# Block 0's root on ScalarE and VectorE, Mish's table loaded behind it, and k, v of batches 2 and 3 on 96 partitions

## The chip, the cores and the metric

The kernel runs on one core of a Trainium2 chip. Measured is the time of one execution on the device in microseconds (us); a comparison takes several executions of each kernel on the same chip. The core's engines are PE (TensorE, matrix products; PEld are its weight loads), DVE (VectorE), ACT (ScalarE), POOL (GpSimd) and SP (SyncE, which here only issues DMAs). Each runs its own instructions strictly in their order and waits on semaphores for the others.

## The reference

A linear attention without softmax gives 2304 rows of 512, and two feed-forward layers follow, the first with Mish, the second with a gated softmax and a normalization:

```python
kv = np.einsum('bhsd,bhse->bhde', k, v)            # batch 4, heads 8, seq 576, dim 64
out = np.einsum('bhsd,bhde->bhse', q, kv)
rms = np.sqrt(np.mean(out * out, axis=-1, keepdims=True) + 1e-06)
x = (out / rms * g_norm)                           # -> 2304 x 512

h = x @ w_in                                       # 512 -> 2048
sp = np.where(h > 20.0, h, np.log1p(np.exp(np.minimum(h, 20.0))))
x = (h * np.tanh(sp)) @ w_out                      # Mish, 2048 -> 512

h = x @ w2_in                                      # 512 -> 1024
e = np.exp(h - np.max(h, axis=-1, keepdims=True))
solu = h * (e / (np.sum(e, axis=-1, keepdims=True) + 1e-09))
ln = (solu - mu) / np.sqrt(var + 1e-06) * g_ln
return ln @ w2_out                                 # 1024 -> 512
```

## The kernel before

The 2304 rows are cut into six blocks of 384 (three tiles `r` of 128 rows each). Float32 operands of the big products are split into two float16 parts, high and low, and a product is three passes over such parts. Three stages follow each other on PE: attention and the first layer (`h_mm` at line 739, with shorter forms from line 833 on), mixed with the layer's second product (line 907), then the second layer (lines 1016 and 1162).

Every piece of work is a task with a key, an engine, a cost and the tasks that it comes after. The table `SEQUENCE` holds the order in which all tasks are written out, which is the order of each engine's instructions; nothing is reordered at run time. `plan.timed` replays the order with the tasks' costs. Where this replay has a gap on PE, `keep_warm` (line 1707) puts in matmuls of 256 columns whose result nobody reads.

The opening, about the first 30 us, is what the change is about. For each batch the eight heads' k and v come in four loads of two heads (`load_pair`, DMAs at line 346), and `kv_pair` (line 379) multiplies them into `kvp`. For batches 0 and 1 (`WIDE`) a head lies on 64 partitions, so that two heads' products run side by side on the halves of the array: 9 rows, 18 matmuls for a pair. For batches 2 and 3 the first 512 of 576 positions lie on 128 partitions (4 rows, 8 matmuls) and the other 64 come by loads of their own (`load_rest`, line 336), on 64 partitions, for 2 matmuls more. `kv_full` (line 384) copies `kvp` to `kvf`, the lower half on ACT and the upper on DVE.

For blocks 0 and 1 a tile then goes through this chain: `t_q` turns q (line 441, PE), `t_xo` multiplies it with `kvf` (line 453, PE), `a_sq` squares (line 497, ACT), `a_ms` sums over a head (line 502, DVE), `a_ep` adds 1e-6 (line 506, POOL), `a_rho` raises to the power -0.5 (line 512, POOL), `a_xf` scales the tile (line 518, DVE), `t_x` turns it (line 461, PE), and `t_xhi` and `t_xlo` (lines 466 ACT and 471 DVE) make the two halves `xT`, which `h_mm` reads. The first products `H0` are done tile by tile, 12 matmuls of 128 columns each.

The weights come in pieces of 512 KB (line 551 for `w_in`) through five buffers `st`. A piece is unpacked by `w_scale` (line 598, ACT), `w_sign` (line 603, POOL), `w_low` (608, DVE), `w_put` (615, DVE), `w_hi` (626, ACT) and `w_lo` (635, DVE). All loads stand in SP's one queue.

## Time and profile before

| what | us |
|---|---|
| median of 3 runs (579.33 to 579.74) | 579.49 |
| profiled execution, its own time | 579.91 |
| span of the profiled execution | 578.1 |
| PE busy in it | 571.4 (99%) |
| DVE, ACT, POOL busy | 441.2, 367.4, 129.3 |

The profile page gives an engine's busy time and its share of the span. The timeline gives each instruction's start and length, the number of equal ones that are merged, and in brackets the engine's idle time before it with what ended it. Float32 matmuls are done in two passes, and products of 64 or 128 columns with different operands then show as two instructions: a pair of heads, 18 matmuls in the program, shows as 36.

### The profile page before, as it was taken

How to read it: one execution, taken by the hardware profiler on the slowest of the kernel's cores; microseconds unless marked ns; L12 is line 12 of the kernel's file. 1: busy time of each engine (PE TensorE's matmuls, PEld its weight loads, DVE VectorE, ACT ScalarE, POOL GpSimd, SP SyncE). 2: the span in 40 equal slices, each digit the busy share in tenths (PEclk: the TensorE clock that was granted, in tenths of full speed). 3: DMA queues.
4: the chain of work that ended last, by engine and by line, in shares of the span. 5: the costliest groups of instructions: out<-in, count | busy, mean ns of one | idle time of the engine just before them, and what ended most of it. 6: DMA issues, size and time to landing. Idle time of an engine off the chain costs nothing.

```text
span 578.1 us, 12245 instructions
## 1 busy us (share of the span) xinstructions
PE 571.4 (99%) x4920; PEld 413.8 (72%) x4920; DVE 441.2 (76%) x745; ACT 367.4 (64%) x636; POOL 129.3 (22%) x185
## 2 busy tenths in 40 slices
PE   8999999999999999999999999999999999999997
PEld 7886666666678877887777787774545557677886
DVE  2899898899958978787573876996575998697851
ACT  2688666675737643364645567774769797888841
POOL 1766422331022301101100101000305305234300
PEclk9999999999999999999999999999999999999999
DMA  8996979928505380225114232281056448676995
GB/s 317 367 237 169 250 207 323 238 84 177 80 1 75 38 248 12 69 93 177 62 73 157 82 128 84 83 289 48 1 137 183 91 74 164 130 163 135 219 221 155
DMA packets 132090, 84.42 MB, mean 146 GB/s; under 512 B 96450, under 2 KB 119362, under 8 KB 131778
## 3 DMA queue, kind: packets, MB, share of 16 engines
q1 hardware_dynamic: 131888, 83.58, 56.7%
q8 instruction: 38, 0.62, 0.4%
q14 instruction: 18, 0.15, 0.1%
q10 hardware_dynamic: 146, 0.07, 0.0%
HBM read 46.67 MB, written 12.06 MB: 102 GB/s over the span
## 4 chain that ended last, share of the span: by engine, by line
PE 96%; DMA 2%; SPq 0%; issue 0%; DVE 0%; ACT 0%; POOL 0%; POOLq 0%; DVEq 0%
PE y L907 33%; PE hp L833 19%; PE h L1016 14%; PE op L1162 13%; PE hp L739 11%; PE kvp L379 2%; PE xo L481 2%; DMA yT<-in_v_dram 1%; DMA w<-ws 1%; PE hp L1707 1%; PE xo L453 1%; PE xTp L461 0%; PE qTp L441 0%; SPq L346 0%; DVE kvf L384 0%
## 5 line engine op out<-in xcount | busy, mean ns | idle before, releaser
L907 PE MATMUL y<-g,w 128*128 128x384 f16 x1152 | 202.5, 326 | 0.0
L907 PEld LDWEIGHTS <-w 128*128 128x128 f16 x1152 | 110.7, 98 | 66.9
L603 POOL TENSOR_SCALAR st<-st 128x512 f32<-128x512 f32 x48 | 41.0, 858 | 211.0 <-ACT P L598 201.0
L1162 PEld LDWEIGHTS <-w 128*128 128x128 f16 x768 | 74.1, 98 | 12.8 <-DMA w<-ws 0.6
L1162 PE MATMUL op<-yT,w 128*128 128x256 f16 (+1 forms) x576 | 72.4, 271 | 0.4 <-DMA w<-ws 0.4
L889 DVE SCALAR_TENSOR_TENSOR g<-m,g 128x768 f16<-128x768 f32 x48 | 45.8, 961 | 15.4 <-ACT g L884 15.1
L739 PEld LDWEIGHTS <-w 128*128 128x128 f16 x480 | 41.2, 98 | 21.3
L833 PEld LDWEIGHTS <-w 128*128 128x128 f16 x576 | 48.4, 98 | 3.7
L833 PEld LDWEIGHTS <-ws 128*128 128x128 f16 x576 | 48.5, 98 | 3.4
L739 PE MATMUL hp<-xT,w 128*128 128x384 f16 (+1 forms) x384 | 49.8, 286 | 0.0
L608 DVE SCALAR_TENSOR_TENSOR st<-st 128x512 int32<-128x512 int32 x48 | 33.5, 706 | 13.7 <-POOL st L603 13.6
L598 ACT ACTIVATE P<-st 128x512 f32<-128x512 f32 x48 | 32.1, 671 | 16.1 <-DMA st<-in_moe_w_in_dram 7.8
L1071 POOL TENSOR_SCALAR small<-small 128x1 f32<-128x1 f32 x18 | 13.0, 720 | 131.6 <-ACT e L1053 131.2
L884 ACT ACTIVATE g<-m 128x768 f16<-128x768 f32 x48 | 39.9, 838 | 3.7 <-PE y L907 3.5
L1016 PEld LDWEIGHTS <-w 128*128 128x128 f16 x210 | 20.6, 98 | 22.3
L1016 PE MATMUL h<-st,w 128*128 128x512 f16 x150 | 35.0, 379 | 0.0
L615 DVE SCALAR_TENSOR_TENSOR P<-P,st 128x512 int32<-128x512 int32 x48 | 33.1, 703 | 1.0
L512 POOL TENSOR_TENSOR rho<-ms,nhalf 128x8 f32<-128x8 f32 x18 | 31.0, 1727 | 1.0
L1162 PE MATMUL op<-ws,w 128*128 128x256 f16 (+1 forms) x192 | 31.1, 271 | 0.0
L850 ACT ACTIVATE st<-hp 128x384 f32<-128x384 f32 x32 | 15.5, 485 | 24.2 <-PE hp L833 24.2
L833 PE MATMUL hp<-xT,ws 128*128 128x192 f16 x336 | 30.8, 246 | 0.0
L1016 PEld LDWEIGHTS <-ws 128*128 128x128 f16 x168 | 16.4, 98 | 17.7
(164 smaller groups left out, 1007.0 us busy)
## 6 DMA issues: line engine op xcount, KB each, us to landing
st<-in_moe_w_in_dram SPq DMA_DIRECT2D x24, 512.0 KB, 6.1
st<-in_moe_w_out_dram SPq DMA_DIRECT2D x24, 512.0 KB, 5.1
w_far<-F SPq DMA_DIRECT2D x15, 256.0 KB, 2.4
qraw<-in_q_dram SPq DMA_DIRECT2D x4, 768.0 KB, 6.2
w_far<-st SPq DMA_DIRECT2D x11, 256.0 KB, 2.6
out_dram<-yT SPq DMA_DIRECT2D x11, 256.0 KB, 2.4
yT<-w_far SPq DMA_DIRECT2D x3, 896.0 KB, 4.9
st<-w_far SPq DMA_DIRECT2D x5, 512.0 KB, 7.1
```

What stands on the lines that cost most here:

```text
L512: nc.gpsimd.tensor_tensor(out=rho, in0=ms, in1=nhalf, op=ALU.pow)
L598: nc.scalar.activation(out=P, in_=v[:, :, 1], func=ACTF.Copy, scale=2.0 ** -111)
L603: nc.gpsimd.tensor_scalar(out=v[:, :, 1], in0=v[:, :, 1], scalar1=0.0, scalar2=1.0, op0=ALU.mult, op1=ALU.mult)
L608: nc.vector.scalar_tensor_tensor(out=v[:, :, 0], in0=v[:, :, 0], scalar=29, in1=v[:, :, 1], op0=ALU.logical_shift_right, op1=ALU.bitwise_or)
L615: nc.vector.scalar_tensor_tensor(out=P.bitcast(I32), in0=P.bitcast(I32), scalar=3, in1=v[:, :, 0], op0=ALU.logical_shift_left, op1=ALU.bit ...
L739: nc.tensor.matmul(out=h_t[b, grp, i][:, t], lhsT=w1[:, f, c, wa], rhs=xT_t[b][:, C * xa + c, t], start=(c == 0 and m == 0), stop=(c == C ...
L833: nc.tensor.matmul(out=p[:, HT * fs:HT * fs + HT], lhsT=lhsT, rhs=x[:, C * xa + 2 * kx + c, HT * n:HT * n + HT], start=(opens and fs == 0 ...
L884: nc.scalar.activation(out=g_t[b, grp][:, 0, 2 * i:2 * i + 2], in_=m_t[b, grp, i], func=ACTF.Copy, scale=64.0)
L889: nc.vector.scalar_tensor_tensor(out=g_t[b, grp][:, 1, j], in0=m_t.pop((b, grp, i)), scalar=64.0, in1=g_t[b, grp][:, 0, j], op0=ALU.mult, ...
L907: nc.tensor.matmul(out=y_t[cc][:, 0:BLK], lhsT=w2[:, grp * G + ii, wa, cc * 128:(cc + 1) * 128], rhs=g_t[b, grp][:, ga, ii], start=(first ...
L1016: nc.tensor.matmul(out=T[p, "2" + bank], lhsT=yF[p][:, x, ya, c], rhs=w3[w][:, c, wa], start=(first and m == 0), stop=(m == 5), skip_group ...
L1162: nc.tensor.matmul(out=T[p, bank][:, lo:hi], lhsT=lnTs[p % 2][:, 8 * x + 4 * la + kk], rhs=w4[kk][:, 7 * HB * wa + HB * w + lo:7 * HB * wa ...
```

## The change

Three things change, and with them the table of the order.

For block 0 the tasks `ep` and `rho` on POOL go. In their place `a_rt` takes the square root on ACT, with 1e-6 as the bias, and `a_recip` the reciprocal on DVE. Block 1 and the blocks after it keep POOL's power. ACT begins with the table for the square root instead of Mish's; a new task `tab` loads Mish's table after the three roots and ahead of the first Mish.

For batches 2 and 3 a head's 576 positions lie on 96 partitions in 6 rows: `load_rest` goes, and a pair is 12 matmuls of 96 partitions.

The table `SEQUENCE` is new up to the middle of the first stage; from there on PE's instructions stand as before. The number of `keep_warm` matmuls is 47 where it was 37.

```diff
 SEQUENCE = """
-442 2164 481 2165 447 443 448 501 514 502 449 527 503 463 450 515 464 516 7 444 465 445 14 466 451 528
+442 2163 0 2164 479 443 447 448 499 512 500 14 501 463 1 449 2 464 450 444 513 15 445 3 514 525 16 7 465
...
+    K1, K2R = 2 * S // 128, S // 96
+    eps = const.tile([128, 1], FP32, name="eps")
...
     def load_pair(b, i):
-        t = raw_of(b, i)[:, 0:2 * K1 * D].rearrange("p (a r d) -> p a r d", a=2, r=K1)
+        t = yT[RAW[b][i]].rearrange("p c a t -> p (c a t)").bitcast(FP32)
+        if b in WIDE:
+            t = t[:, 0:2 * K1 * D].rearrange("p (a r d) -> p a r d", a=2, r=K1)
+        else:
+            t = t[0:96].rearrange("p (a h r d) -> p a h r d", a=2, h=2, r=K2R)
         raw[b, i] = t
         for a, src in enumerate((k, v)):
             s = src[b, 2 * i:2 * i + 2]
...
+            s = s.rearrange("h (p r) d -> (h p) r d", r=K1) if b in WIDE else s.rearrange(
+                "h (p r) d -> p h r d", r=K2R)
+            nc.sync.dma_start(out=t[:, a], in_=s)
...
-        n = K1 if b in WIDE else 5
+        n = K1 if b in WIDE else K2R
         for r in range(n):
             for h in range(2):
...
+                kh, vh = (t[HALF[h], a, r] if b in WIDE else t[:, a, h, r] for a in range(2))
...
+    def a_rt(b, r):
+        rho = at.tile([128, H, 1], FP32, tag="rho", name="rho", bufs=3)
+        nc.scalar.activation(out=rho, in_=ms_t[b, r], func=ACTF.Sqrt, bias=eps)
+        rho_t[b, r] = rho
+
+    def a_recip(b, r):
+        ms_t.pop((b, r))
+        nc.vector.reciprocal(out=rho_t[b, r], in_=rho_t[b, r])
...
-            task(("ep", *u), "G", 0.25, a_ep, u, [("ms", *u)])
-            task(("rho", *u), "G", 1.7, a_rho, u, [("ep", *u)] + ring("rho", 3, ("xf", *u)))
+            if b:
+                task(("ep", *u), "G", 0.25, a_ep, u, [("ms", *u)])
+                task(("rho", *u), "G", 1.7, a_rho, u, [("ep", *u)] + ring("rho", 3, ("xf", *u)))
+            else:
+                task(("rt", *u), "A", 0.22, a_rt, u, [("ms", *u)] + ring("rho", 3, ("xf", *u)))
+                task(("rho", *u), "V", 0.2, a_recip, u, [("rt", *u)])
...
+    task(("tab",), "A", 1.4, nc.scalar.preload_act_table_set, ("mish",), [("rt", 0, r) for r in range(R)])
...
-    nc.scalar.preload_act_table_set("mish")
+    nc.scalar.preload_act_table_set("sqrt_and_others")
+    nc.vector.memset(eps, 1e-6)
```

What the new table does to the order is seen at three places. SP's queue, from its first load on, before (`qraw` is block 0's q, `yT` holds the raw k and v, `st` a weight piece):

```order
L357 DMA qraw<-in_q_dram 128x8x192
L346 DMA yT<-in_k_dram 128x576
L346 DMA yT<-in_v_dram 128x576
L346 DMA yT<-in_k_dram 128x576
L346 DMA yT<-in_v_dram 128x576
L346 DMA yT<-in_k_dram 128x576
L346 DMA yT<-in_v_dram 128x576
L346 DMA yT<-in_k_dram 128x576
L346 DMA yT<-in_v_dram 128x576
L551 DMA st<-in_moe_w_in_dram 128x4x256 x2
```

The same place after the change:

```order
L544 DMA st<-in_moe_w_in_dram 128x4x256
L346 DMA qraw<-in_q_dram 128x8x192
L339 DMA yT<-in_k_dram 128x576
L339 DMA yT<-in_v_dram 128x576
L339 DMA yT<-in_k_dram 128x576
L339 DMA yT<-in_v_dram 128x576
L544 DMA st<-in_moe_w_in_dram 128x4x256
L339 DMA yT<-in_k_dram 128x576
L339 DMA yT<-in_v_dram 128x576
L339 DMA yT<-in_k_dram 128x576
L339 DMA yT<-in_v_dram 128x576
L544 DMA st<-in_moe_w_in_dram 128x4x256
```

One weight piece now stands at the very front and a second between the pairs of batch 0; the third follows directly behind the last pair.

ACT, from q's copies to the second square, before (`P<-st` is the scaling of a weight piece):

```order
L447 ACTIVATE qT<-qTp 128x512 x2
L384 COPY kvf<-kvp 64x4x64
L598 ACTIVATE P<-st 128x512
L447 ACTIVATE qT<-qTp 128x512
L497 ACTIVATE sq<-xo 128x512
L388 ACTIVATE kvr_95<-kvf 64x4x64 x2
L497 ACTIVATE sq<-xo 128x512
```

And after the change, up to the second root:

```order
L431 ACTIVATE qT<-qTp 128x512
L591 ACTIVATE P<-st 128x512 x2
L431 ACTIVATE qT<-qTp 128x512
L591 ACTIVATE P<-st 128x512
L368 COPY kvf<-kvp 64x4x64
L431 ACTIVATE qT<-qTp 128x512
L619 ACTIVATE w_70<-P,gs 128x4x128
L481 ACTIVATE sq<-xo 128x512 x2
L495 ACTIVATE rho<-ms,eps 128x8
L481 ACTIVATE sq<-xo 128x512
L495 ACTIVATE rho<-ms,eps 128x8
```

Three scalings of weight pieces have moved ahead of the copy of `kvf`.

PE, from batch 0's last pairs to the first `H0`, before (`ident` alone is `keep_warm`, eleven times here):

```order
L379 MATMUL kvp<-yT 64x64 x36
L441 MATMUL qTp<-ident,qf 128x128 x4
L453 MATMUL xo<-kvf,qT 128x128 x12
L379 MATMUL kvp<-yT 64x64 x36
L461 MATMUL xTp<-ident,xf 128x128 x4
L1707 LDWEIGHTS ident
L1707 MATMUL hp<-ident 128x256
...
L461 MATMUL xTp<-ident,xf 128x128 x4
L441 MATMUL qTp<-ident,qf 128x128 x4
L379 MATMUL kvp<-yT 64x64 x36
L461 MATMUL xTp<-ident,xf 128x128 x4
L441 MATMUL qTp<-ident,qf 128x128 x4
```

And from `xo` on after the change:

```order
L437 MATMUL xo<-kvf,qT 128x128 x12
L363 MATMUL kvp<-yT 64x64 x18
L425 MATMUL qTp<-ident,qf 128x128 x4
L445 MATMUL xTp<-ident,xf 128x128 x4
L363 MATMUL kvp<-yT 64x64 x18
L425 MATMUL qTp<-ident,qf 128x128 x4
L445 MATMUL xTp<-ident,xf 128x128 x4
L732 LDWEIGHTS w_70
```

The first `H0` now follows the second turned tile, not the third; the third turned tile and batch 1's last two pairs stand between the first `H0`s, and no `keep_warm` is left behind `xo`.

## Rows read from the trace of the kernel before

**Rows 1.** The page: busy time, share of the span, instructions; clock in 40 slices.

```profile
PE 571.4 (99%) x4920; PEld 413.8 (72%) x4920; DVE 441.2 (76%) x745; ACT 367.4 (64%) x636; POOL 129.3 (22%) x185
PEclk9999999999999999999999999999999999999999
```

**Rows 2.** Waits of PE in the whole span: who waited for whom, total, times, longest.

```profile
PE kvp L379 <- DMA yT<-in_v_dram: 0.8, 3, 0.4
PE xTp L461 <- DVE xf L518: 0.6, 2, 0.4
```

**Rows 3.** Timeline of PE, opening: start, length, line, operation, count, idle before.

```profile
7.61 1.26 PE L379 MATMUL kvp<-yT 64*64 64x64 f32 x36
8.81 0.66 PE L441 MATMUL qTp<-ident,qf 128*128 128x128 f32 x4
...
10.74 2.38 PE L379 MATMUL kvp<-yT 64*64 64x64 f32 x72
13.05 0.66 PE L441 MATMUL qTp<-ident,qf 128*128 128x128 f32 x4
14.10 2.94 PE L453 MATMUL xo<-kvf,qT 128*128 128x128 f32 x24 [0.40 <-ACT kvf L384]
16.99 1.26 PE L379 MATMUL kvp<-yT 64*64 64x64 f32 x36
18.44 1.26 PE L379 MATMUL kvp<-yT 64*64 64x64 f32 x36 [0.19 <-DMA yT<-in_v_dram]
...
20.42 1.36 PE L1707 MATMUL hp<-ident 128*128 128x256 f16 x11
22.15 0.66 PE L461 MATMUL xTp<-ident,xf 128*128 128x128 f32 x4 [0.37 <-DVE xf L518]
...
26.51 0.63 PE L461 MATMUL xTp<-ident,xf 128*128 128x128 f32 x4
26.97 0.60 PE L441 MATMUL qTp<-ident,qf 128*128 128x128 f32 x4
27.41 0.83 PE L739 MATMUL hp<-xT,w 128*128 128x128 f16 x12
```

**Rows 4.** Timeline of the other engines, chain from the square to the power.

```profile
15.30 0.60 ACT L497 ACTIVATE sq<-xo 128x512 f32<-128x512 f32 x1 [0.20 <-PE xo L453]
16.01 0.68 DVE L502 TENSOR_REDUCE ms<-sq 128x8 f32<-128x512 f32 x1
17.07 1.67 POOL L512 TENSOR_TENSOR rho<-ms,nhalf 128x8 f32<-128x8 f32 x1
19.18 0.69 DVE L518 SCALAR_TENSOR_TENSOR xf<-xo,rho 128x512 f32<-128x512 f32 x1
```

**Rows 5.** Stretches of the opening: busy time by engine, clock, DMA share, GB/s.

```profile
5.00:10.00 5.00, 5.00 (x74) 4.07 (x74) 1.19 (x3) 1.10 (x2) 0.00 (x0) 1.00 1.04 407
15.00:20.00 5.00, 4.59 (x92) 4.22 (x91) 3.98 (x7) 3.88 (x8) 3.34 (x6) 1.00 1.08 364
35.00:40.00 5.00, 5.00 (x61) 4.21 (x59) 4.96 (x9) 4.15 (x9) 2.40 (x4) 1.00 0.74 259
```

**Rows 6.** Timeline of ACT and DVE, the copy, a scaling, a small copy, q's.

```profile
6.08 0.76 DVE L435 COPY qf<-qraw 128x512 f32<-128x512 f32 x2 [3.38 <-DMA qraw<-in_q_dram]
...
10.84 0.16 DVE L1292 COPY gs<-hp 128x1 f32<-128x1 f32 x1 [2.76 <-PE hp L1289]
...
13.68 0.37 ACT L384 COPY kvf<-kvp 64x256 f32<-64x256 f32 x1 [3.59 <-DVE kvf L384]
13.95 0.66 ACT L598 ACTIVATE P<-st 128x512 f32<-128x512 f32 x1
```

**Rows 7.** Groups of ACT's instructions: the table loads, busy, mean ns, idle before.

```profile
L1695 ACT ACT_TABLE_LOAD x1 | 1.3, 1283 | 0.7 <-PEq L1752 0.7
```

**Rows 8.** Timeline of PE at batch 2's first pair.

```profile
91.59 0.95 PE L379 MATMUL kvp<-yT 128*64 128x64 f32 x20
92.47 0.82 PE L907 MATMUL y<-g,w 128*128 128x384 f16 x4
```

34 lines of the change are left out of this document (4 added, 30 removed), and 186 rows, old and new, of the table SEQUENCE.

## The prediction

> **What bounds the kernel now.** I read the page's busy times first, then the waits of PE, then the timeline of the opening. PE is busy 99% of the span at a granted clock of 0.9 or more in every slice [rows 1], and its waits for operands in the whole run come to little: the two largest kinds for data are 0.8 us for k and v and 0.6 us for the scaled tile, and both lie in the opening [rows 2, 3]. Once the first `H0` has begun at 27.41 us [rows 3] PE is one closed stream, so the end moves with two things only: when that stream gets going, and how much work is in it. A root that is ready sooner is worth nothing by itself. It is worth what it takes out of PE's opening.
>
> In the opening the reader is to see three things. From the first `xo` at 14.10 to the first `H0` at 27.41 [rows 3], 13.31 us pass. The transfers run without a pause, 364 to 407 GB/s [rows 5], so that what PE needs next is there when its turn in the one queue comes. And POOL's power takes 1.67 us [rows 4] for each of three tiles, between a sum and a scaling of 0.7 us each.
>
> **Which work stands where.** By the order of the instructions, PE does the same things ahead of the first `xo` in both kernels (three turns of q, the four pairs of batch 0, the turn of g), apart from fill. Behind it the rest is the same too, with the eleven fill matmuls gone. So I take the first `xo` as the mark: the change in time is the shift of that mark, less the waits and fill that lie behind it now and then no more, plus new waits, plus the change of the work itself.
>
> **What is removed behind the mark.** The 13.31 us hold this work [rows 3]: `xo` 2.89 us (14.10 to 16.99), four pairs of batch 1 at 1.20 us (7.61 to 8.81 is one alone), three turned tiles at 0.46 us (26.51 to 26.97) and two turns of q at 0.44 us (26.97 to 27.41). That is 2.89 + 4.80 + 1.38 + 0.88 = 9.95 us. The other 3.36 us are waits for k and v, waits for the tile that POOL's power holds back, and fill; the stretch of fill alone, from 20.42 to 22.15, is 1.73 us. The whole 3.36 us can go, and no more than that.
>
> **The shift of the mark.** The first `xo` needs both copies of `kvf`. On ACT its copy now stands behind the scaling of the third weight piece, and that waits for its load, which stands behind 768 KB of q, two other pieces of 512 KB and eight loads of k and v of 288 KB. 768 + 3 x 512 + 8 x 288 = 4608 KB must be in. Before, ACT's copy at 13.68 [rows 6] waited for no piece, and only 768 + 8 x 288 = 3072 KB had to come. When are 4608 KB in? PE's wait for v ended just before 18.44 [rows 3], when 768 + 2 x 512 + 12 x 288 = 5248 KB had come. 640 KB less, at 364 GB/s [rows 5] or 355 KB per us, is 1.8 us earlier: 16.6 us. From the other side, q's 768 KB are in at 6.08 [rows 6]; the 3840 KB behind them take 9.7 us at 407 GB/s and 10.8 at 364 [rows 5], which gives 15.8 and 16.9. I take 16.6, since its row is nearest, and keep 15.8 to 16.9. Then 0.05 to start, the scaling at 0.66 less an overlap of 0.10 (0.37 of the copy against 0.27 to the next start), and 0.42 from the copy's start to `xo` (13.68 to 14.10) [rows 3, 6]. The mark comes at 17.6 and not at 14.10: **+3.5 us** (2.7 to 3.8).
>
> **New waits.** Behind the mark PE reaches the first turned tile after `xo`, one pair and one turn of q: 2.89 + 1.20 + 0.44 = 4.53 us. The tile's chain: the square begins 1.20 us behind the mark and takes 0.60, the sum 0.68 [rows 4], so about 2.6. The root stands behind the second tile's square on ACT, which needs the second third of `xo` and ends near 2.8. The trace has no root or reciprocal of 128 x 8. ACT's copy of 0.37 bounds the root from above and DVE's copy of 0.16 the reciprocal from below [rows 6], while 0.68 for a full sum [rows 4] bounds both; the operands are tiny, so I take 0.3 and 0.15, which gives 3.3. DVE then does the second tile's sum, 0.68, ahead of the scaling, 0.69 [rows 4]: 4.7. PE waits about **0.2 us** (0 to 0.7). Batch 1's pairs need 5952 and 6528 KB for the first two, in at 20.4 and 22.0 by the same rate, and PE asks at 20.5 and 22.8; the last two need 7616 and 8192, in at 25.1 and 26.7, asked at 26 and 28. They fit, the first with nothing to spare. DVE is full from 35 to 40 us, 4.96 of 5 [rows 5], but the first piece is now unpacked much earlier, where DVE has work for 1.19 of 5 us [rows 5], so I put nothing there.
>
> Three things that stood ahead of the first `H0` (two pairs and a turned tile) now stand among the `H0`s. A pair alone takes 1.20 us and two together 2.31 (10.74 to 13.05) [rows 3], so the entry and exit cost 0.09 us a time: **+0.3 us**.
>
> **The root itself and the table.** POOL loses 3 x (1.67 + a short addition) us, ACT gains three roots of 0.3 and DVE three reciprocals of 0.15; all of it lies in the chain above. A table load is 1.28 us [rows 7]. The one that is added stands on ACT between the second and the third tile's copy. Behind it wait that copy, three scalings' worth of work and batch 1's copy of `kvf`. PE has four `H0`s of up to 0.83, two pairs, a turned tile and a turn of q [rows 3], 6 us, until batch 1's first `xo`, so 1.28 is hidden; without cover it would cost up to 1.28.
>
> The Trainium skill (ScalarE: Activation LUTs, What ACT_TABLE_LOAD costs) speaks against such a switch: it puts a change to another set at 2.66 us, 1.28 for the load and 1.38 for a drain. The row shows the 1.28, at the start of the program, and no drain behind work. By the page the sum would be up to 0.2 us more, by the row nothing.
>
> **Batches 2 and 3.** A pair takes 0.88 us now (91.59 to 92.47) for 20 rows of two kinds of tile [rows 8]. The new one has 24 rows of one kind. At the pace of further rows in the opening, (2.31 - 1.20) / 36 = 31 ns, plus 0.09, that is 0.83 us; at the mean of the old pair, 0.88 / 20 = 44 ns, it is 1.06. I take the first, because two heads still write different halves of the array and nothing changes between tiles inside a pair. Eight pairs: **-0.4 us** (-0.4 to +1.4). Eight small loads less and sixteen of the same bytes on fewer partitions ride in SP's queue at a time when PE waits for none of them [rows 2]; I put them at nothing.
>
> **Sum.** +3.5 - 3.36 + 0.2 + 0.3 - 0.4 = +0.2 us. The profiled execution took 579.91 us for a span of 578.1; the sum is a difference inside the span, and the median of the runs, 579.49, lies 0.4 below that execution. On the median: 579.7 us. In words: the shorter root is paid with bytes, because the weight pieces that were put ahead of k and v push the whole opening back by what the waits were worth.
>
> **Rivals.** (1) *ScalarE's queue holds the mark longer: slower.* The third piece's load gates the copy of `kvf`, and each us that it lands later than 16.6 is a us of the end. From about 17.5 on the kernel is measurably slower. At a tenth below 364 GB/s, 320 KB per us, the 3840 KB behind q take 12.0 us and it lands at 18.1, +1.5 us on top of the sum, 581.2. Against it stand the rows of 364 and 407 GB/s [rows 5]; for it, that small rows of q and w come first in the queue. (2) *96 partitions do not pair: slower.* If the two heads' matmuls run at 44 ns a row, the last term is +1.4 and the end 581.5. For it speaks only that the trace shows 64 and 128 partitions and never 96. (3) *The gain is whole: faster.* If the load runs at 407 GB/s throughout, the mark comes at 16.8 and PE never waits, -0.8 us, 578.7; to be measurable it needs a little more, as with a third piece that lands at 15.4 or k and v that no longer wait for each other, 578.2. (4) *The root was not what held the first `H0`.* In the order before, `H0` stands behind the third turned tile and two pairs that wait for loads; that is in the forecast already, and by itself it would make the change worth nothing.
>
> **How the numbers follow.** What a measurement of this kernel can tell from no change is about 0.2%, 1.2 us. The forecast, 579.7, with its bounds for the load and the waits (-0.8 to +1.1), lies within that: 70%. Rival 1 has 14%, rival 2 has 8%, both slower; rival 3 has 8%, faster. The range leaves out the upper half of rival 1 and rival 2's end: 578.7 to 581.1.
>
> **What would show it.** Right: in the changed kernel's timeline `xo` begins near 17.6 with ACT's copy released by a scaling that waited for a piece, the first `H0` near 24.9, PE closed from the mark on; a pair of batch 2 takes 0.83 us from start to next start; the second table load lies near 26 us with nothing waiting. Wrong: a mark before 16.5 or after 18.5, new waits of PE behind the first `H0`, above all between 30 and 60 us, a pair of 1 us or more, or a granted clock that falls behind the new waits ahead of the mark.

## The result, and the profile after

The changed kernel is slower: **587.00 us** in the median (585.92 to 589.84) where the kernel before took 579.59 (579.33 to 579.74) beside it, a ratio of **1.0136 [1.0122, 1.0151]**. The profiled execution took 587.98 us, 8.07 more than the profiled one of before. The prediction said 579.7, at most 581.1.

The page of the kernel after, its span, busy times, clock and the shares of its chain of waits:

```profile
span 586.2 us, 12315 instructions
PE 574.2 (98%) x4962; PEld 415.4 (71%) x4962; DVE 443.7 (76%) x749; ACT 368.4 (63%) x640; POOL 123.0 (21%) x179
...
PEclk9999999999999999999999999999999999999998
...
PE 82%; DMA 8%; DVE 7%; issue 1%; ACT 1%; POOL 0%; SPq 0%; ACTq 0%; DVEq 0%; POOLq 0%
```

PE is busy 2.8 us longer than before and the span is 8.1 us longer, so most of the loss is waiting [rows 1]. The last slice shows a granted clock of 8 tenths where all were 9. The waits of PE in the whole span (who waited for whom, total, times, longest):

```profile
PE op L1155 <- DMA w<-ws: 2.7, 1, 2.7
PE xo L437 <- ACT kvf L368: 2.4, 2, 1.4
PE kvp L363 <- DMA yT<-in_v_dram: 1.4, 5, 0.5
...
PE hp L732 <- ACT m L870: 0.8, 2, 0.6
```

The largest one is nowhere near the change. It stands in the last stage, ahead of the last products `op`, for a turned tile `w<-ws`. The second is the `xo` of batches 0 and 1 for `kvf` [rows 2].

The timeline of PE in the opening of after:

```profile
13.03 1.26 PE L363 MATMUL kvp<-yT 64*64 64x64 f32 x36 [0.21 <-DMA yT<-in_v_dram]
14.56 1.26 PE L363 MATMUL kvp<-yT 64*64 64x64 f32 x36 [0.27 <-DMA yT<-in_v_dram]
...
18.37 2.94 PE L437 MATMUL xo<-kvf,qT 128*128 128x128 f32 x24 [1.41 <-ACT kvf L368]
21.41 1.26 PE L363 MATMUL kvp<-yT 64*64 64x64 f32 x36
...
25.75 0.83 PE L732 MATMUL hp<-xT,w 128*128 128x128 f16 x12
...
33.06 2.05 PE L437 MATMUL xo<-kvf,qT 128*128 128x128 f32 x16 [0.97 <-ACT kvf L368]
...
48.27 0.87 PE L465 MATMUL xo<-kvr,qT 128*64 128x128 f16 x24
```

The mark is at 18.37 (before 14.10), the first `H0` at 25.75, which is 1.66 earlier than before [rows 3]. Behind it stands a new wait, at 33.06. ACT and DVE there, in their timelines:

```profile
17.41 0.66 ACT L591 ACTIVATE P<-st 128x512 f32<-128x512 f32 x1 [4.72 <-DMA st<-in_moe_w_in_dram]
17.97 0.35 ACT L368 COPY kvf<-kvp 64x256 f32<-64x256 f32 x1
20.95 0.30 ACT L495 ACTIVATE rho<-ms,eps 128x8 f32<-128x8 f32 x1
...
27.67 1.28 ACT L1198 ACT_TABLE_LOAD   x1
28.97 0.60 ACT L450 ACTIVATE xT<-xTp 128x512 f16<-128x512 f32 x1
```

```profile
21.28 0.20 DVE L500 RECIPROCAL rho<-rho 128x8 f32<-128x8 f32 x1 [0.37 <-ACT rho L495]
```

ACT idles 4.72 us for the third weight piece, scales it, and only then copies `kvf`. Root and reciprocal take 0.30 and 0.20 us. The three stretches of the opening and of the end (columns as in [rows 5]):

```profile
5.00:10.00 5.00, 4.30 (x59) 3.36 (x57) 0.76 (x2) 1.15 (x2) 0.64 (x1) 1.00 1.07 368
15.00:20.00 5.00, 3.59 (x52) 3.19 (x48) 2.19 (x4) 2.45 (x5) 0.71 (x2) 1.00 1.09 358
...
574.50:578.50 4.00, 3.95 (x24) 2.94 (x25) 0.00 (x0) 0.38 (x1) 0.00 (x0) 0.64 0.87 237
```

The DMA engines are as full as before (1.07 against 1.04) and move less: 368 GB/s against 407 [rows 5]. At the end the granted clock falls to 0.64 in the mean, a mixture of its two levels, 1.2 and 2.4 GHz. The end of PE's timeline, before and then after:

```profile
568.17 1.16 PE L1162 MATMUL op<-yT,w 128*128 128x256 f16 x9 [0.35 <-DMA w<-ws]
```

```profile
574.55 1.16 PE L1155 MATMUL op<-yT,w 128*128 128x256 f16 x9 [2.70 <-DMA w<-ws]
...
576.11 2.12 PE L1155 MATMUL op<-yT,w 128*128 128x256 f16 x9
```

From this product to the start of the last matmul 6.54 us pass before (568.17 to 574.71) and 8.20 after (574.55 to 582.75). Nine matmuls of this kind take 1.16 us and, with the clock down, 2.12.

**Where the 8.07 us lie.** Matching PE's instructions of the two traces one by one (below, the *shift* is how much later the same instruction starts): the stream is 2.77 us late at the first `xo` from `kvr` (48.27 against 45.50), 4.04 from 170 us on and unchanged to 510, then 6.4 behind the wait of 2.70 and 8.05 at the end. So half of the loss is the opening and the first stage, and half the last 15 us.

### The profile page after: what moved, and what is told of

Its sections match the earlier page's. It is cut to its first block, busy times and chain, and to the rows that moved or that the text cites. A ratio compares the mean times of both kernels' runs of the same rounds, so it can differ in the third digit from the quotient of the medians.

```text
span 586.2 us, 12315 instructions
## 1 busy us (share of the span) xinstructions
PE 574.2 (98%) x4962; PEld 415.4 (71%) x4962; DVE 443.7 (76%) x749; ACT 368.4 (63%) x640; POOL 123.0 (21%) x179
## 4 chain that ended last, share of the span: by engine, by line
PE 82%; DMA 8%; DVE 7%; issue 1%; ACT 1%; POOL 0%; SPq 0%; ACTq 0%; DVEq 0%; POOLq 0%
PE y L900 28%; PE hp L826 19%; PE h L1009 14%; PE op L1155 14%; PE hp L732 4%; DMA st<-in_moe_w_in_dram 4%; DMA st<-in_moe_w_out_dram 2%; DVE st L601 1%; PE xo L465 1%; DMA yT<-in_v_dram 1%; DMA w<-ws 1%; DVE w L628 1%; PE xo L437 1%; DVE P L608 1%; DVE xf L511 1%
## 5 line engine op out<-in xcount | busy, mean ns | idle before, releaser
L596 POOL TENSOR_SCALAR st<-st 128x512 f32<-128x512 f32 x48 | 37.9, 795 | 218.3 <-ACT P L591 203.8
L732 PEld LDWEIGHTS <-w 128*128 128x128 f16 x480 | 40.8, 98 | 22.3 <-issue 1.2
L1009 PEld LDWEIGHTS <-w 128*128 128x128 f16 x210 | 20.5, 98 | 22.3
L843 ACT ACTIVATE st<-hp 128x384 f32<-128x384 f32 x32 | 15.5, 485 | 24.8 <-PE hp L826 24.8
L826 PE MATMUL hp<-xT,ws 128*128 128x192 f16 x336 | 30.8, 246 | 0.0
L1009 PE MATMUL h<-st,ws 128*128 128x512 f16 x120 | 28.0, 379 | 0.0
```

What stands on the lines that cost most here:

```text
L596: nc.gpsimd.tensor_scalar(out=v[:, :, 1], in0=v[:, :, 1], scalar1=0.0, scalar2=1.0, op0=ALU.mult, op1=ALU.mult)
L732: nc.tensor.matmul(out=h_t[b, grp, i][:, t], lhsT=w1[:, f, c, wa], rhs=xT_t[b][:, C * xa + c, t], start=(c == 0 and m == 0), stop=(c == C ...
L826: nc.tensor.matmul(out=p[:, HT * fs:HT * fs + HT], lhsT=lhsT, rhs=x[:, C * xa + 2 * kx + c, HT * n:HT * n + HT], start=(opens and fs == 0 ...
L843: nc.scalar.activation(out=h_e(b, grp, n), in_=p[:, 0:BLK], func=ACTF.Copy)
L1009: nc.tensor.matmul(out=T[p, "2" + bank], lhsT=yF[p][:, x, ya, c], rhs=w3[w][:, c, wa], start=(first and m == 0), stop=(m == 5), skip_group ...
```

## The experiments

All runs, in the order in which they ran; *shift* as above, in the middle of the run (170 to 510 us), *end wait* PE's wait for the last `w<-ws`; these two and the starts of the first `xo` and the first `H0` are of the profiled execution. Ratios are to runs of the kernel before on the same chip.

| kernel | median (range) | ratio | shift | first `xo` | first `H0` | end wait |
|---|---|---|---|---|---|---|
| before | 579.59 (579.33–579.74) | | 0 | 14.10 | 27.41 | 0.35 |
| after | 587.00 (585.92–589.84) | 1.0136 [1.0122, 1.0151] | +4.04 | 18.37 | 25.75 | 2.70 |
| again | 588.36 (586.25–589.24) | 1.0145 [1.0119, 1.0170] | +4.02 | 18.33 | 25.72 | 2.6 |
| only96 | 581.87 (581.19–583.53) | 1.0041 [1.0025, 1.0058] | +1.68 | 14.17 | 28.10 | none |
| late4 | 584.69 (584.03–586.05) | 1.0089 [1.0074, 1.0104] | +3.65 | 17.69 | 31.06 | 0.6 |
| copyfirst | 587.96 (587.70–589.04) | 1.0146 [1.0130, 1.0161] | +4.99 | 16.93 | 25.91 | 2.7 |
| before2 | 579.66 (579.29–579.92) | 0.9998 [0.9988, 1.0007] | +0.03 | 13.94 | 27.44 | 0.2 |
| after2 | 587.88 (586.92–588.35) | 1.0137 [1.0122, 1.0152] | +5.61 | 19.21 | 27.18 | 2.4 |
| thirdwork | 587.78 (585.70–590.10) | 1.0126 [1.0098, 1.0154] | +5.72 | 16.91 | 26.41 | 3.1 |
| rootonly | 584.85 (583.04–586.27) | 1.0085 [1.0061, 1.0110] | +1.96 | 14.54 | 29.24 | 3.1 |
| slot | 583.70 (582.67–586.29) | 1.0063 [1.0045, 1.0081] | +5.83 | 19.15 | 26.79 | 0.8 |
| pad32 | 584.27 (582.14–586.21) | 1.0078 [1.0047, 1.0109] | +0.73 | 14.40 | 28.15 | 3.0 |
| pad64 | 582.13 (581.87–583.26) | 1.0046 [1.0030, 1.0062] | +0.67 | 14.54 | 28.08 | 1.6 |
| rootslot | 580.99 (580.73–581.05) | 1.0022 [1.0012, 1.0032] | +1.18 | 13.93 | 28.59 | 0.3 |
| oldroot | 584.06 (583.90–584.18) | 1.0077 [1.0062, 1.0092] | +4.34 | 17.68 | 26.57 | 0.2 |
| warmslot | 583.11 (582.57–583.87) | 1.0061 [1.0046, 1.0076] | +3.62 | 17.98 | 25.74 | 0.3 |
| thirdslot | 584.18 (583.04–586.55) | 1.0084 [1.0060, 1.0108] | +3.27 | 16.53 | 25.92 | 0.2 |
| rootbest | 584.18 (581.99–584.77) | 1.0066 [1.0044, 1.0089] | +3.68 | 14.05 | 28.76 | 1.5 |
| afteract | 587.59 (585.61–589.01) | 1.0134 [1.0115, 1.0154] | +4.29 | 18.17 | 25.57 | 2.5 |
| beforeact | 579.61 (579.23–580.19) | 1.0000 [0.9991, 1.0009] | +0.09 | 13.86 | 27.50 | 0.3 |

### again: k and v of batches 2 and 3 loaded as before

The changed kernel with the third part of the change undone, and with `load_rest` and its tasks back in an order that is otherwise after's:

```diff
-        n = K1 if b in WIDE else K2R
+        n = K1 if b in WIDE else 5
...
+            task(("ldr", b), "S", 1.6, load_rest, (b,), free + ([("kv", 1, 3)] if b == 2 else []), LAND)
```

> The changed kernel, with k and v of batches 2 and 3 loaded and multiplied as in the kernel before (four rows of 128 partitions and a shared rest), everything else as changed. Its own time tells what the 96 partitions are worth. Theory A (the +4.0 us that the stream has by 160 us comes from the opening, the layout costs next to nothing): first xo at 18.4 us, first H0 at 25.8, the stream from 170 to 480 us still 3.5 to 4.5 us behind the kernel before. Rival B (the layout makes part of it): 1 us or more of the 4 is gone. The end is open: the changed kernel waited 2.7 us for its last transposed tile and ran 1.6 us longer behind that. If that comes from the other number of DMA packets that the layout gives (128888 against 132090), the wait is gone here and the time is about 583.5; if it comes with the late stream or from chance, it stays, 585.5 to 588.

588.36 us, shift 4.02 against 4.04. In the new order the 96 partitions cost nothing and bring nothing that shows in the time. They do what the prediction took them to do: the first pair of batch 2 in after lasts 0.85 us from start to next start, where it took 0.88 [rows 8].

```profile
91.39 0.92 PE L363 MATMUL kvp<-yT 96*64 96x64 f32 x24
92.24 2.12 PE L732 MATMUL hp<-yT,w 128*128 128x384 f16 x12
```

### only96: the 96 partitions alone, in the order of before

```diff
-        n = K1 if b in WIDE else 5
+        n = K1 if b in WIDE else K2R
```

> The kernel before with nothing changed but k and v of batches 2 and 3 on 96 partitions. The prediction had -0.4 us for this by itself (0.83 us a pair against 0.88); the trace of the changed kernel shows 0.85 a pair, which gives -0.2, 579.3. If the number of DMA packets makes the wait at the end, it appears here too, 2 to 4 us, 581.5 to 583.5, with the stream at 480 us still where the kernel before has it. If 96 partitions hurt the transfers of the weights between 60 and 110 us, PE shows new waits there.

Slower by 0.41% [0.25, 0.58], not faster. The pairs are as short as in after, but the last pair of batch 3 waits for its v (PE's timeline):

```profile
143.14 0.92 PE L362 MATMUL kvp<-yT 96*64 96x64 f32 x24 [1.14 <-DMA yT<-in_v_dram]
```

The other 0.69 us, by which the first `H0` is late already (28.10 against 27.41), lies in the opening, where SP's issue of one load of k (at 13.37) took 3.91 us instead of 3.17. No part of the edit touches that load, and why it took longer stays open.

### late4: a late mark alone

The kernel before with 37 matmuls of `keep_warm` ahead of the first `xo`:

```diff
+        if key == ("xo", 0, 0):
+            keep_warm(37, h_open(h_line[0]))
```

> The kernel before with 37 matmuls of fill ahead of the first xo, about 4.0 us at 0.11 us each, and nothing else. It asks whether a stream that is only later has the wait at the end. If the end depends on nothing but the work behind it: everything is 2 to 4 us later (less what the waits of the opening take up: up to 3.4 us of waits and fill stand behind the mark), the last wait stays 0.3 to 0.4 us, and the time is 579.5 plus the shift that the stream has at 480 us. If a late stream by itself makes the wait, it is 2 us or more here.

The mark moves by 3.59 us (14.10 to 17.69), and the shift in the middle is 3.65: a late mark reaches the end one to one. But the end wait is 0.6, not 2.7. So a late stream by itself does not make a wait of that size; something else does.

### copyfirst: the copy of `kvf` ahead of the third scaling

The changed kernel with two of ACT's rows moved:

```diff
 L431 ACTIVATE qT<-qTp 128x512
-L591 ACTIVATE P<-st 128x512
 L368 COPY kvf<-kvp 64x4x64
 L431 ACTIVATE qT<-qTp 128x512
+L591 ACTIVATE P<-st 128x512
```

> The changed kernel with ACT's copy of kvf of batch 0 (and its third copy of q) ahead of the scaling of the third weight piece, and nothing else moved. Theory A (that scaling, which waited for its piece until 17.4 us, holds the mark): the first xo begins at 16.4 instead of 18.4, and the stream at 170 us is 1 to 2 us less behind, so 1 to 2 us are gained, 585 to 586 with the wait at the end as it was, 581.5 to 582.5 without it. Rival (the third weight piece is needed for the first H0 anyway): xo at 16.4, but the first H0 still near 25.8 and the stream as late as before.

The mark comes 1.44 us earlier (16.93), and the first `H0` is no earlier (25.91 against 25.75). DVE's timeline shows who holds it now:

```profile
18.77 0.70 DVE L601 SCALAR_TENSOR_TENSOR st<-st 128x512 int32<-128x512 int32 x1 [1.63 <-POOL st L596]
...
19.58 0.69 DVE L608 SCALAR_TENSOR_TENSOR P<-P,st 128x512 int32<-128x512 int32 x1
20.19 0.68 DVE L486 TENSOR_REDUCE ms<-sq 128x8 f32<-128x512 f32 x1
```

The third piece's work stands in DVE's queue too, ahead of the first tile's sum. It waits 1.63 us for the piece, by way of POOL's sign, and the sum waits behind it; the first scaled tile is ready at 22.71. PE meanwhile waits 1.25 us for v of batch 1, until 21.35, and comes to turn the tile at 23.25. That ACT's queue alone holds the opening is out.

### before2 and after2: both kernels once more

> The kernel before, once more and unchanged. It tells how far two profiled executions of one kernel agree in three places: the opening (first H0 at 27.41 us in the first profile; with only 96 partitions, whose opening is the same program, 28.10), the stream from 170 to 480 us, and SyncE's issue times of the transposed tiles at the end (some of them took 1.3 us more in one kernel than in another). If the opening and the end vary by chance, first H0 lies anywhere from 27.2 to 28.3 and the last wait from 0 to 1 us, and the median is again within 0.3 us of 579.6. If they are a property of the program, both agree to 0.1 us.

> The changed kernel, once more and unchanged. Property of the program: first H0 25.7 to 25.8, the stream 4.0 us behind from 170 us on, the last wait 2.6 to 2.8 us, each issue of a transposed tile at the end within 0.1 us of the first profile. Chance: the stream agrees to some tenths, the last wait lies anywhere from 0 to 4 us.

The kernel before repeats: its medians in all comparisons lie between 579.54 and 579.88, and its stream agrees to 0.03 us from 170 us on. The changed kernel has the same ratio and not the same opening: in after2 the fourth pair waited 1.86 us for v, the clock behind it was 0.76 from 15 to 20 us (1.00 in after), and `xo` took 3.70 us instead of 2.94. How its loads fall made a difference of 1.6 us in the opening of these two executions.

### thirdwork: all of the third piece's work behind the first tile's

As copyfirst, with the scaling also behind the first square on ACT, and the piece's rows moved on DVE too (shown: DVE):

```diff
-L601 SCALAR_TENSOR_TENSOR st<-st 128x512
-L608 SCALAR_TENSOR_TENSOR P<-P,st 128x512
 L486 TENSOR_REDUCE ms<-sq 128x8
...
 L511 SCALAR_TENSOR_TENSOR xf<-xo,rho 128x512
+L601 SCALAR_TENSOR_TENSOR st<-st 128x512
```

> The changed kernel with the work on the third weight piece moved behind work on the first tile: on ACT its scaling behind the copy of kvf, the third copy of q and the first square, on DVE its two steps behind the first and the second scaled tile. The loads stay in their order. Theory A (the third piece holds the opening in two queues, ACT's ahead of the copy of kvf and DVE's ahead of the first sum; moving it in one alone gave an xo at 16.93 and the first H0 still at 25.91): xo at 16.4 to 16.9, the first scaled tile 1.5 to 2 us earlier than 22.07, the first H0 at 23.7 to 24.5, the stream at 170 us 1 to 2.5 us less behind than 4.0. Rival B (the loads of batch 1 hold it, the pair that came at 21.35 in the run before): first H0 at 25.2 to 25.9. Rival C (the opening gains, but DVE and ACT give it back before 60 us, since their work until then is the same): first H0 early, the stream at 48 us still 2.5 to 2.8 us behind.

587.78 us: no gain with both queues freed. But this run still carries what rootonly and the four kernels after it show, so it settles nothing about the queues; thirdslot, below, has the same order without that.

### rootonly: the new root in the order of before

The first part of the change alone, with its lines as in the diff above and the loads of before.

> The kernel before in its own order, with nothing but the root of batch 0 on ScalarE and the reciprocal on VectorE and the table load behind the third root. It asks what the root is worth without the new order of the loads. Theory A (in the order before, the last two pairs of batch 1, whose loads land near 23.6 and 25.0 us, stand ahead of the first H0 whatever the root takes): first H0 27.0 to 27.6, 579.2 to 579.8 us. Rival B (the root held it): the two waits for the scaled tile and the fill go, first H0 at 25.5 to 26.5, 578 to 578.7. Rival C (the table load stands in ACT's queue where a copy is due): a new wait of up to 1.28 us, 580 to 581.

Slower by 0.85% [0.61, 1.10], with a shift of only 1.96 us in the middle and an end wait of 3.1. None of after's loads, no late mark, and yet after's end. What rootonly shares with after is the root, the table load, and one more line, the new constant tile `eps`.

### slot, pad32, pad64, rootslot: where the tiles lie

`eps` holds one number on each partition, and takes 32 bytes of it behind `zero`. Every tile that is placed behind it on that side of the memory begins 32 bytes later: in the built programs `w1` lies at 17696 instead of 17664 and `yT` at 83232 instead of 83200. Before, these begin at multiples of 256. The tiles of the other side (`st`, `g`, `ws` among them) do not move; they lie 224 bytes behind a multiple of 256 in before and after alike. Four kernels tell the place from the work. In slot `eps` shares the 32 bytes of `zero`, so nothing moves:

```diff
-    zero = const.tile([128, 1], FP32, name="zero")
-    eps = const.tile([128, 1], FP32, name="eps")
+    zeps = const.tile([128, 2], FP32, name="zeps")
+    zero, eps = zeps[:, 0:1], zeps[:, 1:2]
```

rootslot is rootonly with the same edit. pad32 is the kernel before with a tile that nobody reads (pad64 the same with 16 columns, 64 bytes):

```diff
+    pad = const.tile([128, 1], FP32, name="pad")
...
+    nc.vector.memset(pad, 0.0)
```

> The changed kernel with the constant eps in the 32-byte slot that the tile zero has anyway, and nothing else changed. As a tile of its own eps moved every tile behind it in its side of SBUF (both weight tiles, the tiles that k and v are loaded into, the ones that the last transposed tiles are read from and written to) by 32 bytes: they started at multiples of 256 bytes before and start 32 bytes behind them since. Theory A (that move slows the DMA packets of all these tiles): the third weight piece lands near 16.6 us instead of 17.4, first xo 17.4 to 17.8, the last wait falls from 2.4 to 2.7 us to less than 1, and the time is 579.5 to 582.0. Rival B (the root, the table load or the order make the end wait; the place in memory does nothing): first xo 18.4 to 19.2, last wait 2 to 3 us, 586 to 588.

> The kernel before with one unused tile of 4 bytes behind zero, set once by VectorE at the start, and nothing else: every tile behind it starts 32 bytes later. Theory A (the move slows the packets): k and v land later in the opening, first H0 28.0 to 29.5 instead of 27.41, a last wait of 2 us or more, 582 to 586. Rival B: all as before, 579.3 to 580.0.

> As the run before it, with a tile of 64 bytes: everything behind starts 64 bytes later, still off a multiple of 256. If the packets want 64-byte boundaries: as the kernel before, 579.3 to 580.0. If they want a boundary of 256 bytes (the Trainium skill, DMA: Bandwidth & Descriptors, How a descriptor splits into AXI transactions, has reads fetched in pieces of 256 bytes from boundaries of 256): slower like the run with 32, 582 to 586. If an additional tile and its setting are enough by themselves, also slower.

> The kernel before in its own order with the root on ScalarE and VectorE, as in an earlier run (584.85 us, first H0 29.24), but with eps in the slot of zero, so that no tile moves. It tells what the root alone is worth. Theory A (the 4 to 7 us of that run came from the move): first H0 27.0 to 27.6, last wait under 0.6 us, 579.0 to 579.8. Rival B (the root in this order costs by itself: ScalarE and VectorE hold it behind their weight work, PE waited 2.4 us for scaled tiles): the end as before, but first H0 28 to 29, 580.5 to 581.5.

One unused tile of 32 bytes makes the kernel before slower by 4.65 us (584.27 against 579.62 beside it); 64 bytes cost 2.5. That such a tile is also set once does not matter: `eps` is set in slot and rootslot too. Taking the displacement away gives 3.9 us back in rootonly (584.85 to 580.99) and 3.3 to 4.2 in after (587.00 and 587.88 to 583.70). SP's timeline shows the mechanism in one instruction, the turn of a part of `w1` into `w2` by DMA (`w<-w`), issued while nothing else moves. One line each of before, pad32, pad64, after and slot:

```profile
418.92 1.68 SPq L1138 DMA_TRANSPOSE w<-w  x1
```

```profile
419.67 2.10 SPq L1139 DMA_TRANSPOSE w<-w  x1
```

```profile
419.60 2.06 SPq L1139 DMA_TRANSPOSE w<-w  x1
```

```profile
422.95 2.02 SPq L1131 DMA_TRANSPOSE w<-w  x1
```

```profile
424.76 1.69 SPq L1131 DMA_TRANSPOSE w<-w  x1
```

The same bytes take 1.68 us from tiles at multiples of 256 and 2.02 to 2.10 from tiles displaced by 32 or 64. In the trace's records of single packets, the 2048 packets of 256 bytes of this turn take 17.9 ns in the mean in before and in slot, and 21.2 in after, pad32 and pad64, +18%. Not every packet is longer: the median is 18.0 in all five. In the displaced ones about a quarter takes longer than that, some 175 of them 40 ns and more, where before has none.

A turn of `ws`, later and also alone, tells which end of the transfer matters. It writes into `w2` like the other, and reads a tile that lies 224 bytes behind a multiple in every kernel. Before, then pad32:

```profile
432.88 3.63 SPq L1138 DMA_TRANSPOSE w<-ws  x1
```

```profile
433.61 3.66 SPq L1139 DMA_TRANSPOSE w<-ws  x1
```

It does not change, and its packets, 3072 of 256 bytes, take 21.9 ns in the mean in both: already in before as long as the displaced ones of `w<-w`. By this comparison a displaced source is enough to lengthen a turn, and a displaced destination adds nothing to that; a displaced destination alone does not occur in these turns.

Larger packets lose less: in the opening those of 2304 bytes, k and v, which are written into the displaced `yT`, go from 93 ns to 96 and 98 (medians, pad32 and after). And the opening's rate from 5 to 10 us, 407 GB/s before, falls to 391 in pad32 with nothing else changed; with after's loads it is 379 in slot and 368 in after:

```profile
5.00:10.00 5.00, 3.70 (x71) 2.95 (x69) 1.19 (x3) 1.07 (x2) 0.00 (x0) 1.00 1.06 391
```

```profile
5.00:10.00 5.00, 4.71 (x63) 3.84 (x63) 0.76 (x2) 1.15 (x2) 0.41 (x1) 1.00 1.07 379
```

At the end of the program the DMA engines of after have some 38,000 packets of 256 bytes between 500 and 570 us; their mean is 24.1 ns, 22.7 in before. An estimate from these: 38,000 x 1.4 ns over 16 engines is 3.3 us. It is a rough one, since the mean differs from kernel to kernel with the tiles in place too (22.3 to 23.4; displaced 23.7 to 24.6): against slot, which has after's order and 23.2, it is 2.0 us, and for pad32 against before 4.2. The issues on SP say it by kind of turn. Added up from 500 us on, those of `w<-w`, which read a tile that moved, take 12.4 us in before and 15.8 in pad32, 11.6 in rootslot and 15.5 in rootonly, 14.1 in slot and 17.4 in after. Those of `w<-g` and `w<-ws`, which read tiles that did not move, take 30.2 and 29.8, 31.9 and 30.8, 33.8 and 33.2.

The last turned tile is issued at 568.55 instead of 561.59, 6.96 us later where the stream is 4.04 late; the other 2.9 us come from SP's queue ahead of it. PE runs into it and stands, and the clock does the rest. pad32's end, of PE's timeline and of its stretch:

```profile
571.55 2.10 PE L1163 MATMUL op<-yT,w 128*128 128x256 f16 x9 [2.98 <-DMA w<-ws]
```

```profile
571.50:575.50 4.00, 3.95 (x19) 2.85 (x20) 0.00 (x0) 0.39 (x1) 0.00 (x0) 0.50 0.85 235
575.50:579.50 4.00, 4.00 (x30) 3.18 (x29) 0.76 (x2) 0.39 (x1) 0.00 (x0) 0.75 0.00 0
```

Before has 1.00 from 568 to 572 us; 0.50 is the lower of the two levels, 1.2 GHz. In this execution (586.21, the longest of its four and 6.30 over before's) 0.73 is the shift, 2.63 the longer wait, and the remaining 2.9 the matmuls behind it at 0.50 and 0.75. Behind pad64's wait of 1.6 the clock stays at 1.00 (570 to 574 us) in its profiled execution, and its time is the smaller for it.

The Trainium skill (DMA: Bandwidth & Descriptors, How a descriptor splits into AXI transactions) says that a transaction that reads must start at a 256-byte boundary, so that the bytes ahead of a displaced start are fetched too and cost beats. An estimate from its table: 256 bytes displaced by 32 would take 9 beats instead of 8, by 64 ten, by the 224 of `ws` fifteen. The direction agrees, and so do that 64 does not help and that a displaced source is enough. The size does not: the turn takes 2.10 and 2.06 us, about the same for 32 and 64, the packets from `ws` are 22% longer in the mean and not nearly twice as long, and three quarters of the packets are no longer at all.

### oldroot: after's order with the old root

The changed kernel with `ep` and `rho` on POOL again, Mish's table first, and no `eps`:

```diff
-    eps = const.tile([128, 1], FP32, name="eps")
...
+            task(("ep", *u), "G", 0.25, a_ep, u, [("ms", *u)])
+            task(("rho", *u), "G", 1.7, a_rho, u, [("ep", *u)] + ring("rho", 3, ("xf", *u)))
```

> The changed kernel's order (weight pieces ahead of k and v, k and v of batches 2 and 3 on 96 partitions) with the old root by GpSimd's power, the Mish table loaded at the start, and no tile for eps, so no tile moves. Theory A (the order costs by itself and the root gives something back within it): the chain of each tile is 1.3 to 1.6 us longer, first H0 28 to 28.6 instead of 26.8, PE waits for scaled tiles, 584 to 585.5, slower than the 583.7 of the changed kernel in the same places. Rival B (the root or its table load costs): faster than 583.7, 580 to 583.

584.06 us, 4.5 over before beside it. The new loads and order cost this much without any new root; against slot (583.70) and warmslot, which has fill besides (583.11), the root would be worth 0.4 to 1.0 us, which the intervals do not separate.

### warmslot: slot with fill ahead of the fourth pair

slot's profiled execution shows after2's opening: a wait of 1.85 us, then a low clock (PE's timeline, then the stretch):

```profile
15.84 1.41 PE L363 MATMUL kvp<-yT 64*64 64x64 f32 x36 [1.85 <-DMA yT<-in_v_dram]
...
19.15 3.36 PE L437 MATMUL xo<-kvf,qT 128*128 128x128 f32 x24
```

```profile
15.00:20.00 5.00, 4.16 (x49) 3.75 (x50) 2.04 (x4) 2.25 (x4) 1.62 (x2) 0.68 1.06 368
```

```diff
+        if key == ("kv", 0, 3):
+            keep_warm(14, h_open(h_line[0]))
```

> The changed kernel with no tile moved, and 14 matmuls of fill (1.5 us) ahead of the fourth pair of batch 0, where PE waited 1.85 us. Theory A (the wait lets the granted clock fall, and the first xo and the turns of q behind it run at it: xo 3.36 us for 2.94, a turn of q 1.11 for 0.66): granted clock 1.00 from 15 to 20 us, xo 2.9 us long, the stream at 170 us 1 to 1.8 us less behind than 5.83, 582 to 583. Rival B (the fall comes by chance or does not matter, since xo waits for ACT's copy anyway): stream 5 us or more behind, 583.5 to 584.5.

The stretch in warmslot:

```profile
15.00:20.00 5.00, 5.00 (x71) 4.50 (x69) 2.27 (x4) 2.71 (x5) 1.65 (x3) 1.00 1.08 371
```

With work in the wait the clock stays at 1.00, `xo` takes 2.94 us and the shift is 3.62 instead of 5.83. The median gains 0.6 us, which the intervals do not separate. Not every execution of slot seems to lose the clock: the mean granted clock of its four is 0.996, 0.997, 1.000 and 1.000, and 1.000 in all four of warmslot.

### thirdslot: thirdwork with the tiles in place

The edits of thirdwork and slot together.

> The changed kernel with no tile moved and the work on the third weight piece behind work on the first tile, in ACT's and in DVE's queue (with moved tiles this gave xo at 16.91, but first H0 at 26.41 and the stream 5.72 us behind). Theory A (the third piece holds the opening; with moved tiles the loads of batch 1 came too late to show it): xo at 16 to 16.6, first H0 24 to 25.3, the stream 1.5 to 3 us behind, 580.5 to 582.5. Rival B (the bytes hold it: batch 1's k and v stand behind three pieces and land when they land): first H0 25.5 or later, the stream 4 us or more behind, 583 to 585.

The mark is at 16.53, so both queues are free of the third piece. The first `H0` is still at 25.92, and PE's timeline says why:

```profile
20.92 1.26 PE L363 MATMUL kvp<-yT 64*64 64x64 f32 x36 [1.23 <-DMA yT<-in_v_dram]
...
25.92 0.83 PE L732 MATMUL hp<-xT,w 128*128 128x128 f16 x12
```

PE now waits 1.23 us for batch 1's v, and 0.66 us of fill that the planner put ahead of `H0` take the rest of the gain. Freeing both queues leaves the opening about where it was: what is loaded ahead of k and v is paid at the one wait or at the other.

### rootbest: before's loads, the new root, and an order made for it

rootslot with the opening's work on ACT and DVE rearranged so that the first two roots stand behind no weight work, and with the third turned tile ahead of batch 1's last pairs on PE (shown: ACT; DVE alike):

```diff
 L498 ACTIVATE sq<-xo 128x512
 L512 ACTIVATE rho<-ms,zeps 128x8
-L608 ACTIVATE P<-st 128x512
-L498 ACTIVATE sq<-xo 128x512
-L636 ACTIVATE w_69<-P,gs 128x4x128
+L498 ACTIVATE sq<-xo 128x512
 L512 ACTIVATE rho<-ms,zeps 128x8
+L608 ACTIVATE P<-st 128x512
```

> The kernel before, its loads in their order, no tile moved, with the root on ScalarE and VectorE and the work around it put in order for it: roots ahead of the copies and scalings of weights on ACT, sums, reciprocals and scaled tiles ahead of the weight steps on DVE, the third turned tile ahead of the last pairs of batch 1 on PE. In the old order this root gave 580.99 us and PE waits of 2.6 us for scaled tiles. Theory A (batch 1's last pairs and the weight pieces, not the root, set the first H0): no wait for scaled tiles any more, but waits for v; first H0 27 to 27.6, 579.2 to 580. Rival B (the root is worth what it takes off): first H0 25.5 to 26.8, 577.9 to 579.

584.18 us, worse than rootslot (580.99). In rootslot PE waits for the scaled tiles, since root and reciprocal stand behind weight work in the queues of ACT and DVE; in rootbest that wait is gone, the first `H0` waits for the weights themselves, and the clock behind that wait is 0.66. The waits of rootslot, and PE's timeline and a stretch of rootbest:

```profile
PE xTp L462 <- DVE xf L528: 2.6, 3, 1.1
```

```profile
28.76 0.28 PE L749 MATMUL hp<-xT,w 128*128 128x128 f16 x2 [1.51 <-ACT w L636]
```

```profile
30.00:35.00 5.00, 5.00 (x52) 4.94 (x50) 4.97 (x9) 4.73 (x10) 2.54 (x4) 0.66 1.12 245
```

In rootbest PE is through with all that stands ahead of the first `H0` at 27.25 (28.76 less the wait of 1.51), 0.16 us before the old start at 27.41. So in this order scaled tiles that are ready in time bring the first `H0` next to nothing: batch 1's last pairs and what follows them hold it (the v of the last pair came at 25.09 in before). Whether another order gains more was not tried.

### afteract and beforeact: stores out of SP's queue at the end

Both kernels with three stores of the end issued by ACT, so that the last turned tiles stand behind fewer stores in SP's queue (of after):

```diff
-            (nc.scalar if half == 2 else nc.sync).dma_start(out=o[n % R][:, c], in_=osb(p, t)[lo:hi, c])
+            (nc.scalar if half == 2 or (p, t) in ((4, 0), (5, 0), (5, 1)) else nc.sync).dma_start(
```

> The changed kernel as it is (tiles moved), with the output's stores (4, 0), (5, 0) and (5, 1), four DMAs that stand between the last transposed tiles on SyncE and take 0.6 to 1.2 us of its queue each, issued from ScalarE instead. Theory A (the end hangs on SyncE's queue, which is busy without a pause from 551 to 572 us): the last transposed tile is issued 2.5 to 3.5 us earlier against PE's stream, the last wait of 2.4 to 2.7 us is gone or under 0.5, the clock does not fall there, and the time is 583.2 to 585.2. Rival B (the tiles wait for VectorE or for the DMA engines, not for the queue): the last wait stays above 1.5 us, 586 to 588.

> The kernel before with the same three stores issued from ScalarE. Its last wait is 0.2 to 0.4 us and is the only thing there to gain: Theory A 579.1 to 579.4 us. If ScalarE's issue holds up a copy that PE waits for: 579.7 to 580.5.

No difference to after or to before. SP's timeline of afteract at the end (start, length, line, operation, count):

```profile
551.64 10.25 SPq L1131 DMA_TRANSPOSE w<-g  x3
561.99 6.87 SPq L1131 DMA_TRANSPOSE w<-w  x2
568.97 3.70 SPq L1131 DMA_TRANSPOSE w<-ws  x1
```

The last tile is issued at 568.97 instead of 568.55. The three turns `w<-g` now take 10.25 us where they took 8.14 in after (9.32 in again, with the stores in their places): what the queue no longer spent on stores it spent on the turns. This one run speaks against the stores and for the transfers as the bound there, which agrees with the displaced tiles as the cause. VectorE is not it: DVE has written the last part of that tile by 561.39 in after, 7 us before the issue.

### What stays open

That displaced tiles make the packets longer, and that their place alone costs 4 us, is shown (pad32, slot, rootslot). That the end wait is those packets' sum rests on the issues of `w<-w`, 3.3 to 3.9 us more in three pairs of kernels, on the rough estimate, and on late4 and afteract, which speak against the late stream and the stores. What the displaced destinations cost, `yT` in the opening above all, was not tried apart, and neither was a kernel with `g` and `ws` at multiples of 256. rootbest has an end wait of 1.5 with its tiles in place, at a shift at which late4 has 0.6; its packets of 256 bytes at the end are at the upper end of the kernels in place, 23.4 ns, and so are late4's, 23.3. Why is not known, so displaced tiles are not the only way to that wait. What makes 64 bytes cheaper than 32 in the end (2.5 and 4.65 us), when the turn alone takes the same, is open too; behind pad64's shorter wait the clock stayed up. About 0.5 us of after's shift between 48 and 170 us was not placed.

## Why the prediction was wrong, point by point

**The step that failed** is the first one: once the first `H0` has begun, PE "is one closed stream, so the end moves with two things only". Nothing in the sum stood for the end. Before, PE reached the last `w<-ws` 0.35 us ahead of the tile, a wait so small that it was not read; after, 2.35 us more, and 1.66 at a low clock behind it: 4.0 of the 8.07 us. The edit that caused it was in the diff, `eps = const.tile([128, 1], ...)`, and the prediction has no term for it: it costed the instructions of the root and not the place of the tile they read. The other half is the sum for the opening itself, +0.2 us, where 4.04 were measured by 170 us; its terms are below.

**The sum, term by term** (profiled executions):

| term | predicted | measured in after |
|---|---|---|
| shift of the mark | +3.5 (2.7 to 3.8) | +4.27 |
| removed behind it | −3.36 | −3.36 |
| waits from the mark to 48 us | +0.2 (0 to 0.7) | +0.97 |
| entries and exits of split work | +0.3 | +0.89 |
| waits behind 48 us | none | +1.02 |
| pairs of batches 2 and 3 | −0.4 | −0.24 (8 x 0.03) |
| not placed | | +0.5 |
| the end: wait and clock | none | +4.0 |
| sum | +0.2 | +8.05 |

- **The mark** was sized 0.8 too small. The third piece's scaling began at 17.41, not 16.65. The rate was taken from before [rows 5], and part of the difference is the displaced tiles, as with them in place (slot) the scaling began at 17.06. Rival 1 named the mechanism, with 14%, and put its price for a load at 18.1.
- **The new wait** was looked for at the first turned tile and came at 33.06, for batch 1's `kvf`: DVE's copy of it stands at 32.18 behind weight work and ACT's at 32.64. The prediction costed DVE's load at nothing because the first piece is unpacked earlier; DVE was still busy 4.91 of 5 us from 30 to 35.
- **Entries**: the same matmuls from the mark to 48 us take 28.93 us instead of 28.04, though only three pieces of work were counted as newly split at 0.09 each. Part of this was in the 3.36 us: the timeline of before names 2.72 of them, the waits for v (0.76 together), one of 0.23 for a scaled tile and the stretch of fill (1.73). The other 0.64 are pieces that last longer than their price, as the pair from 25.09 to 26.51, 1.42 us for 1.20, and the sum took them as removed.
- **Behind 48 us** three waits of 0.57, 0.18 and 0.27 us show. The text named new waits behind the first `H0` as what would make it wrong, and gave them no price.
- **Right**: root and reciprocal took 0.30 and 0.20 (0.3 and 0.15 were taken); the table load lies at 27.67, 1.28 us long, and nobody waited; no drain is seen around it, since the operation ahead ended at 27.65 and the next began at 28.97, 1.32 us in all where the Trainium skill (ScalarE: Activation LUTs, What ACT_TABLE_LOAD costs) has 2.66. The pair takes 0.85 against 0.83, so rival 2 is out. Rival 4, that the root was not what held the first `H0`, is what rootbest shows, for the order that it has.
- **The clock** was named as a risk ahead of the mark. It came true there in after2 and slot, and with a higher price at the end.

With the tiles in place (slot, warmslot) the change costs 3.5 to 4.1 us and not 0.2: even without the missed term the kernel would have been slower, by the mark, the waits and the entries together. No kernel here was faster than before.

## What to carry to other kernels

A new constant is also a new address for every tile behind it: where a kernel leans on DMAs of small packets, compare the tiles' addresses before and after an edit, those that DMAs read from first, and put a small constant into a slot that is already there. Here `g` and `ws` were displaced all along; whether moving them pays was not tried. A stream that is called closed has to be followed to its last wait; the waits that are nearly zero before, such as 0.35 us here, are the ones that open. And work that is loaded early is paid with bytes by what it overtakes, and a second time in every engine's queue where its processing stands ahead of something urgent.
